# Two layers of spectral filter and mixer on one core: a half table negated on VectorE instead of loaded, layer 1's transform copies walked the other way, and three new instruction orders

## The chip, the cores and the metric

The kernel runs on one NeuronCore of a Trainium2 chip. The metric is the device time of one launch in microseconds (us). Before the change it was 348.33 us, the median of three runs (348.26 to 348.41). The engines are called as in the profile: PE (TensorE, the matrix engine; PEld is its weight load), DVE (VectorE), ACT (ScalarE), POOL (GpSimd) and SP (SyncE, which here only issues DMAs).

## What is computed

The input `x` has 2048 rows of 512 channels. The program applies block A, block B, block A, block B, with the same weights each time and a layer norm and a residual around each block.

```python
def _A_ref(x, w_r, w_i):
    X = rfft2(x, axes=(-2, -1))
    y = irfft2(X * (w_r + 1j * w_i), s=(S, D), axes=(-2, -1))       # S = 2048, D = 512
def _B_ref(x, w1, w2, w3, w4):
    h = gelu(layernorm(x) @ w1)                                     # w1: 512 x 512
    # the four quarters of h's channels are moved by +1, -1, +2, -2 rows
    x1 = x + shifted(h) @ w2                                        # w2: 512 x 512
    return x1 + gelu(layernorm(x1) @ w3) @ w4                       # w3: 512 x 1792, w4: 1792 x 512
x = x + _A_ref(layernorm(x));  x = x + _B_ref(layernorm(x))         # and both once more
```

## The kernel before

`x` stays on the chip as 16 rows q of a tile of 128 partitions by 512 channels (row number = 16 p + q). A layer is one block A and one block B. It has these stages, and in the order strings each step is a letter, the number of the piece, sometimes the engine that copies (V for DVE, A for ACT) and, behind a point, the bank of PSUM that it starts in:

- **p transform.** `Q` scales the table T by a row's 1/std, `O` multiplies two rows with it (`over_p`, or `over_p_plain`), `G` copies the result to the tile V. Of layer 1 this is done in `first_front`, together with the statistics (`s`, `i`, `f`, `S`, `J`), while `x` is still being loaded; of layer 2 it is done while layer 1's last products run.
- **The front of block A**, on 16 blocks b taken in ten units of one or two blocks: `d` (`over_d`, transform over the channels; `t` is its copy to the tile TV), `q` (`over_q`, with the tables TL; `x` is its copy to X), `p` (`weigh`, on DVE: X times the filter W, to PB), `b` (`back_q`, with the tables TR; `m` is its copy into the tile hT). Only after the last `m` can `D` start.
- **The back of block A:** `D` (`back_d`; `Y` is its copy), `P` (`back_p`), `a` (`add_x`, on DVE: adds x and sums), `s` (squares, ACT), `r`, `e`, `i`, `c` (statistics of four rows, on POOL, ACT and DVE), `n` (normalise), `T` (a DMA transpose of two rows, issued by SP).
- **Block B:** `v` (w1) with gelu `h` (ACT), `u` (w2 on shifted columns), `f` (DVE add), `k` (squares), `E` (residual), `R`, `o` (normalise, DVE or ACT), `U` (DMA transpose), `w` (w3) with gelu `g`, and `W` (w4) with `A` (add on DVE). In layer 1, `B`, `j`, `S`, `J` are the next layer's statistics, and `L` (`permute`, DVE) re-sorts W for layer 2. In layer 2 `y` (`store`) issues a row's store on SP.

Every engine runs its instructions in the order of the program, and the program is written out by hand in three strings: ORDER_0 for `first_front`, ORDER_A for layer 1, ORDER_B for layer 2. What an engine waits for follows from the data, from the bank of PSUM that a product is written to (it must have been copied out), and from buffers: TV and Y share four, X has two, so that `x` of one unit waits for `p` of the unit two before.

The tables come by DMA. POOL's queue (`load_rest`, L179 to L197) loads FA, TL and half 0 of TR, issues a DMA that doubles a quarter of W, waits on a one-element copy (`gate`, L191) for the last scaled table of `first_front`, then makes the second form of TL in two halves (`turn_TL`: a scaling of 1.66 us and a copy of 0.75 us for each), with three more doublings and half 1 of TR between and behind them. `back_q` multiplies planes k and k+1 of TR, so it needs the three planes A, B and -A of the blocks' half: blocks 0 to 7 use half 0, blocks 8 to 15 half 1. Half 0 comes with two planes, and DVE makes the third (`N0`, `negate`); half 1 is loaded with all three.

Layer 1 keeps TV with the two halves h interleaved (f h), as W comes; layer 2, after the permutes, keeps it as (h f). So layer 1's copy `t` has to interleave.

Of the kernel before, what the change touches and what calls it, by code (L numbers as in the profile page):

```python
# [28 lines left out]
def dft_tables():  # L29

    p = np.arange(P)
    pair = lambda j, s: (j if s == 0 else 64 - j) if j else 32 * s
# [6 lines left out]
    T = T.reshape(P, P)  # L50
# [104 lines left out]
def load_all(K, A_x, A_w_r, A_w_i, B_w1, B_w2, B_w3, B_w4):  # L155
# [24 lines left out]
    def load_rest(after):  # L180
        q = nc.gpsimd
        load_TL = lambda k: q.dma_start(K.TL[:, 0, 8 * k:8 * k + 8], dram["TL"][:, 8 * k:8 * k + 8])
        load_TR = lambda k: q.dma_start(K.TR[:, 0:2 + k, 16 * k:16 * k + 16], dram["TR"][:, 0:2 + k, 16 * k:16 * k + 16])
# [636 lines left out]
P6.2 s3 D2.0 s0 s1 a7 s7 a6 s6 D5.3 D4.6 r0 e0 Y2V P4.5 Y5A Y4A i0 n0V n1V P5.0 a4 s4 a5 s5 P11.2 D7.4 r1 P10.6 T0 Y7A  # L820
P8.3 e1 n3V n2V c1 T1 a11 a8 i1 D6.0 Y6A n5V P9.4 s11 P14.7 n4V n6V a9 n7V T2 P15.5 P12.3 a10 s8 a15 s9 a14 s10 P13.0
L0 v0.1 h0 a12 a13 v1.5 h1 T3 r2 c2 v3.4 n11V s12 c0 n10V T5 n8V n9V h3 s15 v2.3 h2 u0.5 L8 u3.0 u2.7 f0 L2 s14 f3
u1.5 f1 s13 r3 n12V n14V n15V f2 T4 v5.2 n13V h5 v4.1 u4.5 f4 E1 h4 u7.6 u6.1 f7 E3 u5.4 T7 k1 k0 f6 f5 k3 k2 E5 R0 c3
T6 v7.5 h7 u15.7 E0 v6.0 h6 E6 E4 u8.4 k7 o0V k5 o1V f15 E2 k6 o2V u10.3 o3V f10 k10 u12.7 u11.0 f8 u14.1 f14 U0 U1
u9.2 f9 k9 k8 w2.4 g2 f12 L9 E9 k4 R1 f11 k11 R2 w5.6 E11 g5 w4.2 g4 w1.0 u13.4 E8 o8V g1 o9V w3.5 g3 f13 E10 o10V
w0.1 g0 E7 o4A o7V w6.3 g6 W2.2 z0 o5V o6V A2 W3.7 A3 W1.6 A1 B1 W0.2 U3 U4 U2 E14 A0 w8.6 L13 B3 j3 g8 k14 o11V w12.1
g12 U5 w13.6 g13 w7.3 g7 w9.6 g9 k15 w10.3 g10 w18.0 w15.3 E12 g18 g15 w14.6 g14 w16.0 L11 w11.3 g11 g16 B2 W6.2 E13
W4.0 A6 w20.5 k13 L5 A4 B4 L12 W7.0 g20 w17.4 k12 R3 g17 o13A W5.1 A5 w19.5 g19 W9.2 o12V U6 j1 A7 B7 L15 j7 E15 j2 L7
o15V B6 W8.1 j6 B0 B5 j5 L3 W10.7 j0 S0 A10 B10 o14A U7 A9 j10 w25.4 g25 B9 Q2 j4 j9 A8 B8 L1 S1 Q1 Q4 w24.6 g24 W11.0
# [10 lines left out]
s5 a7 s7 a3 r1 P2.0 a2 P0.7 a0 s3 P1.3 a1 s2 e1 i1 n4V D5.4 D7.1 D4.6 Y5A P11.3 P10.0 n5V D6.4 n7V n6V s0 s1 r0 Y7A e0  # L840
Y4V P8.6 P9.2 T2 P14.1 a10 i0 c1 n2V n3V Y6A s10 a11 n1V P15.0 n0A s11 a9 a8 s9 s8 c0 r2 T3 P13.7 a13 P12.5 a12 T1
v3.3 h3 v2.6 h2 s12 n10V T0 v1.2 n8V n9V T4 v0.4 s13 n11V h1 u3.7 a14 T5 h0 a15 u1.6 f1 u0.0 s15 u2.4 f2 s14 r3 n14V
n15V T7 n12V v5.2 h5 v4.1 h4 u4.5 n13V E1 k1 u6.4 f3 E3 f0 E0 u7.3 k2 u5.7 k3 k0 c2 f7 T6 v6.2 h6 v7.1 h7 E2 f5 u13.6
R0 u12.0 E7 o2V u14.7 o3V o1V f6 o0V c3 f12 U0 f13 u15.2 f15 k15 f4 f14 E14 E15 E6 k13 k12 u9.0 f9 u10.1 k14 U1 w2.4
g2 w4.6 k4 f10 R3 k10 E13 w0.1 g0 w6.3 E12 o12A g4 w1.1 g1 g6 w3.5 g3 w5.1 g5 u11.5 E4 k5 f11 W2.3 E11 o13V o14A k7 U6
o15A k11 W1.4 A1 k6 R1 u8.2 A2 f8 k9 k8 R2 o6V U7 w25.6 g25 w22.3 o4V E10 o10A g22 E5 o5V w21.0 W3.2 A3 g21 w24.5 g24
o11V E9 w26.0 g26 o7V E8 w27.2 w23.5 U2 o8A g23 g27 W0.0 A0 y0 y2 W12.6 W14.7 A14 A12 W15.3 y3 o9V U3 w8.5 g8 y1 w11.1
g11 U4 A15 y15 w12.3 w10.0 g12 g10 U5 W13.7 A13 w7.1 w16.3 g16 g7 y13 w20.5 g20 w9.0 g9 w13.2 g13 W7.4 A7 y12 W4.6
# [33 lines left out]
```

## Time and profile before

The profiled execution took 348.26 us. Its span, the time from first to last recorded instruction, is 346.5 us, which leaves 1.76 us around it. It is 0.07 us below the median.

| stretch, us from the span's start | what runs | PE busy | DVE busy | ACT busy |
|---|---|---|---|---|
| 0 to 18.7 | loads of x, statistics, p transform of layer 1 | 16.16 | 14.40 | 13.93 |
| 18.7 to 38.4 | front of block A, layer 1 | 19.19 | 17.82 | 17.46 |
| 38.4 to 53.1 | back of block A, layer 1 | 14.47 | 12.37 | 12.48 |
| 53.1 to 179.4 | block B, layer 1, up to the last w4 product | 125.81 | 73.32 | 58.39 |
| 179.4 to 183.5 | rest of layer 2's p transform | 4.02 | 3.92 | 3.38 |
| 183.5 to 203.1 | front of block A, layer 2 | 19.16 | 18.01 | 17.26 |
| 203.1 to 218.4 | back of block A, layer 2 | 14.51 | 11.14 | 14.24 |
| 218.4 to 343.1 | block B, layer 2 | 124.16 | 36.48 | 54.81 |
| 343.1 to 346.5 | last add and store | 0 | 0.40 | 0 |

Busy times of PE overstate: the end of a matmul is modelled, and one that streams 512 columns is written down with 379 ns where the next one starts 216 ns later. In the two stretches of block B the matmuls follow each other at that distance; in the other stretches three engines hand work round, and the chain of waits, which goes back from the last instruction to whatever released each step, changes its engine every microsecond or so. The clock that was granted to PE is 1.0 in every stretch.

### The profile page before, as it was taken

The page shows a single profiled execution, that of the slowest core. Times are in us where ns is not written, and L with a number is a line of the kernel's source. Part 1 is how long each engine was busy: PE and PEld are TensorE (multiplying, and loading weights), DVE is VectorE, ACT ScalarE, POOL GpSimd, SP SyncE. Part 2 cuts the span into 40 slices and gives each one's busy share as a digit, 9 for nine tenths or more (in the row PEclk, how much of TensorE's full clock was granted, in tenths as well). Part 3 has the DMA queues.
Part 4 walks back from the last instruction along what each step waited for, and adds up shares of the span by engine and source line. Part 5 has one row for each costly group of instructions (what it writes and reads, how often), then busy time and mean ns, then how long its engine had stood idle before and what let it go on. Part 6 is the DMA issues. An engine that isn't in the chain of part 4 may idle for free.

```text
span 346.5 us, 5563 instructions
## 1 busy us (share of the span) xinstructions
PE 337.5 (97%) x2116; PEld 190.0 (55%) x2134; DVE 187.9 (54%) x452; ACT 192.0 (55%) x342; POOL 65.2 (19%) x158
## 2 busy tenths in 40 slices
...
GB/s 265 290 328 246 359 132 111 80 63 7 49 45 30 0 2 0 55 38 1 0 2 0 2 2 53 95 88 50 23 2 61 30 45 104 19 30 17 45 23 53
DMA packets 45337, 24.64 MB, mean 71 GB/s; under 512 B 34944, under 2 KB 42240, under 8 KB 45312
## 3 DMA queue, kind: packets, MB, share of 16 engines
q1 hardware_dynamic: 43904, 20.00, 23.6%
...
q14 instruction: 9, 0.07, 0.1%
...
## 4 chain that ended last, share of the span: by engine, by line
PE 80%; DVE 8%; ACT 5%; DMA 4%; issue 2%; DVEq 0%; SPq 0%; ACTq 0%
PE ps L686 28%; PE ps L706 27%; PE ps L635 8%; PE ps L651 8%; PE ps L511 3%; DVE x_state L603 3%; DMA xT<-xn 2%; ACT V L152 2%; PE ps L583 2%; DVE PB L554 2%; PE ps L535 1%; DMA x_state<-in_A_x_dram 1%; DVE hT L150 1%; ACT X L152 1%; DMA T<-tab_T 1%
## 5 line engine op out<-in xcount | busy, mean ns | idle before, releaser
L693 ACT ACTIVATE gT<-ps 128x1024 bf16<-128x1024 f32 x56 | 56.3, 1022 | 93.9 <-PE ps L686 93.7
L686 PE MATMUL ps<-xT,w 128*128 128x512 bf16 x448 | 99.3, 379 | 0.1
L706 PE MATMUL ps<-w,gT 128*128 128x512 bf16 (+1 forms) x464 | 97.8, 366 | 0.6
L712 DVE TENSOR_TENSOR x_state<-ps,x_state 128x512 bf16<-128x512 f32 (+1 forms) x34 | 22.1, 657 | 108.6 <-PE ps L706 106.9
L706 PEld LDWEIGHTS <-gT 128*128 128x128 bf16 x476 | 46.5, 98 | 49.9
L686 PEld LDWEIGHTS <-w 128*128 128x128 bf16 x448 | 43.7, 98 | 52.9 <-DMA xT<-xn 0.6
L659 DVE SCALAR_TENSOR_TENSOR xn<-xn,ln_c,ps 128x512 bf16<-128x512 bf16 x32 | 23.2, 744 | 21.4 <-PE ps L651 13.1
L635 PE MATMUL ps<-xT,w 128*128 128x512 bf16 x128 | 28.8, 379 | 0.9 <-DMA xT<-xn 0.9
L651 PE MATMUL ps<-w,hT 128*128 128x512 bf16 x122 | 28.6, 379 | 0.3
L285 ACT ACTIVATE junk<-xn 128x512 bf16<-128x512 bf16 x32 | 19.7, 619 | 10.1 <-DVE xn L659 10.1
L642 ACT ACTIVATE hT<-ps 128x512 bf16<-128x512 f32 x32 | 18.1, 601 | 11.8 <-PE ps L635 11.8
L603 DVE SCALAR_TENSOR_TENSOR x_state<-ps,x_state 128x512 bf16<-128x512 f32 x32 | 20.5, 686 | 5.1 <-PE ps L595 5.1
L273 DVE BATCH_NORM_STATS2 ln_st<-x_state 128x6 f32<-128x512 bf16 (+1 forms) x31 | 20.2, 667 | 3.6 <-DMA x_state<-in_A_x_dram 3.2
L635 PEld LDWEIGHTS <-w 128*128 128x128 bf16 x128 | 12.4, 98 | 16.0 <-issue 1.6
L291 POOL TENSOR_SCALAR ln_mv<-ln_s 128x4 f32<-128x4 f32 x16 | 4.9, 304 | 85.3 <-DVE x_state L603 73.2
L651 PEld LDWEIGHTS <-hT 128*128 128x128 bf16 x128 | 12.5, 98 | 15.1
L554 DVE TENSOR_TENSOR PB<-X,W 128x2048 bf16<-128x2048 bf16 (+1 forms) x20 | 19.6, 1010 | 0.7 <-ACT X L152 0.5
L285 ACT ACTIVATE xn<-x_state 128x512 bf16<-128x512 bf16 x32 | 19.9, 624 | 0.2 <-DVE x_state L603 0.2
L293 POOL TENSOR_TENSOR ln_mv<-ln_s,ln_t 128x4 f32<-128x4 f32 x16 | 3.5, 217 | 75.4 <-ACT junk L285 70.0
L583 PE MATMUL ps<-G,hT 128*128 128x256 bf16 x128 | 15.4, 272 | 0.9 <-DVE hT L150 0.8
L565 PE MATMUL ps<-TR,PB 128*128 128x128 bf16 x256 | 16.1, 219 | 0.1
L565 PEld LDWEIGHTS <-PB 128*128 128x128 bf16 x256 | 14.8, 98 | 1.5 <-issue 1.2
...
## 6 DMA issues: line engine op xcount, KB each, us to landing
w<-in_B_w_dram SPq DMA_DIRECT2D x2, 1792.0 KB, 12.1
...
```

The source lines that it names most:

```text
L285: K.nc.scalar.activation(out, src, ACT.Square, bias=0.0, scale=D ** -0.5, accum_out=self.s[:, i, 1:2])
L554: nc.vector.tensor_tensor(t, X.pop(u)[:, 0:2 * n].unsqueeze(1).to_broadcast([P, 2, 2 * n, 256]), K.W[:, :, 2 * u:2 * u + 2 * n, 1:257], op ...
L565: nc.tensor.matmul(oh, lhsT=pab[u][:, k, 2 * (b - u) + h, F * P:(F + 1) * P], rhs=K.TR[:, k:k + 2, 2 * b + h], start=(k == 0), stop=(k == 1))
L583: nc.tensor.matmul(o[:, i, e * 256:(e + 1) * 256], lhsT=M[:, F, e, 2 * m + i, :], rhs=K.G[:, F, e, :], start=(F == 0 and e == 0), stop=(F ...
L603: nc.vector.scalar_tensor_tensor(K.x[:, q, :], ps.pop(("P", q)), 1.0, K.x[:, q, :], op0=ALU.mult, op1=ALU.add, accum_out=ln[g].s[:, i, 0:1])
L635: nc.tensor.matmul(o[:, i], lhsT=K.w1[:, t, j * P:(j + 1) * P], rhs=xT[g][:, :, t, :], start=(t == 0), stop=(t == 3))
L651: nc.tensor.matmul(o, lhsT=K.hT[:, j, st:st + P], rhs=K.w2[:, j, :], start=(j == 0), stop=(j == 3))
L659: nc.vector.scalar_tensor_tensor(xn[:, q, :], xn[:, q, :], ln[q // 4].c[:, q % 4:q % 4 + 1], ps.pop(("u", n)), op0=ALU.mult, op1=ALU.add, ...
L686: nc.tensor.matmul(o[:, i], lhsT=K.w3[:, c, t * P:(t + 1) * P], rhs=xT3[g][:, :, c, :], start=(c == 0), stop=(c == 3))
L693: nc.scalar.activation(gT[g][:, 2 * j:2 * j + 2, :], ps.pop(("w", k)), ACT.Gelu_apprx_tanh, bias=0.0, scale=1.0)
L706: nc.tensor.matmul(o, lhsT=gT[g][:, t, i * P:(i + 1) * P], rhs=K.w4[:, t, d], start=(t == 0), stop=(t == 13))
L712: nc.vector.tensor_tensor(x, ps.pop(("W", n)), x, op=ALU.add)
```

## The change

Five things differ; the tiles, the matmuls and their number are the same.

1. The table TR is stored with two planes, and half 1 is loaded with two planes (512 KB, was 768 KB).
2. Layer 1 has a second `negate`, `N1`, on DVE, that makes the third plane of half 1.
3. Layer 1's copy `t` walks its elements in the order (h f) instead of (f h). The source in PSUM is then read in sequence and the destination in SBUF is written at every second element; before, the source was read at a jump of 128 elements and the destination written in sequence. What is stored where is the same.
4. All three order strings are replaced.
5. As the new ORDER_0 ends with `Q15A`, the last scaled table, for which POOL's `gate` waits, is made by ACT; before, it was `Q14V`, on DVE.

The number of zero matmuls ahead of the first p transform (35, `WAKE`) and the halving of one row of w4 by columns in each layer (`HALVES`) are the same in both kernels.

```diff
-    TR = np.concatenate([TR, -TR[:, :1]], axis=1)
...
-        load_TR = lambda k: q.dma_start(K.TR[:, 0:2 + k, 16 * k:16 * k + 16], dram["TR"][:, 0:2 + k, 16 * k:16 * k + 16])
+        load_TR = lambda k: q.dma_start(K.TR[:, 0:2, 16 * k:16 * k + 16], dram["TR"][:, :, 16 * k:16 * k + 16])
...
-            copy(K, tv[u][:].rearrange("p n (e f h) -> p (n e) f h", e=2, h=2),
-                 src.rearrange("p n (e h f) -> p (n e) f h", e=2, h=2), eng)
+            copy(K, tv[u][:].rearrange("p n (e f h) -> p (n e) h f", e=2, h=2),
+                 src.rearrange("p n (e h f) -> p (n e) h f", e=2, h=2), eng)
...
 ORDER_0 = """
-s0 s2 i0 s3 s1 i2 i3 f0 s4 S0 J0 i4 s5 Q1V Q0V Q3V Q2V s7 s6 i7 i6 s9 s11 O0 G0A f1 i9 S1 J1 s8 O1 G1A Q6A s10 Q7A i11
-O3 i8 i10 Q5A s13 s12 Q4A O2 S2 J2 i13 Q10V G3A i12 Q9V s15 Q11A O5 S3 Q8A s14 i15 G2A O4 i14 S4 J3 Q12V G5A J4 Q15A
-Q13V O6 Q14V G6A G4V O7 G7V O8 G8V G8A
+s0 s2 s3 i0 i2 i3 s1 f0 S0 s4 J0 Q2V Q3V O1 i4 s5 s7 s6 Q1A Q0A i7 i6 G1A f1 S1 O0 G0A s11 s10 i11 J1 Q6A i10 s8 s9
+Q7A Q4A i8 i9 s13 Q5A s12 S2 J2 i13 i12 Q10V O3 G3A Q11A O2 Q8V O5 Q9A s15 s14 S3 J3 i15 i14 G2A S4 Q13V Q12V J4 Q14V
+G5A Q15A O4 O6 G6A G4V O7 G7V O8 G8A G8V
 """
 ORDER_A = """
-X4.1 N0 d0.3 t0A d2.5 d1.7 t1A d4.0 t4A q0.2 x0A t2V q1.4 x1V p1 d10.6 d6.4 p0 t6V q2.1 t10A q4.6 x2A p2 x4A d12.3
-b1.0 q6.1 p4 q10.6 t12A m1V b3.3 m3V x6A d8.4 d14.2 d15.0 x10A b5.6 t8A q8.4 p6 t14V t15A q12.0 b2.7 p10 m2V q14.2 m5A
-x8A x12A q15.4 b0.6 m0A b10.7 m10A b4.1 m4A p8 b6.0 p12 m6V x14A p14 b11.7 x15A b9.1 p15 b13.6 m11A m9V m13A b7.3
-b12.5 m12A b8.2 m8A b14.7 m14A m7V b15.5 m15A m15V D1.1 Y1V D0.5 D3.3 P2.7 a2 P3.2 a3 Y0A P0.1 a0 Y3A P7.4 P1.7 a1 s2
...
-w21.2 g21 Q6 w22.6 j8 A11 L4 Q0 Q7 B11 j11 g22 L10 O0.3 w26.1 L14 g26 S2 Q11 G0A Q3 w23.6 w27.0 Q9 G0V g23 O1.2 G1A
-Q10 G1V g27 W12.5 A12 O3.0 B12 W15.6 j12 Q5 G3A G3V A15 O2.2 G2A B15 Q8 j15 G2V S15 J15 Q15 W13.5 A13 B13 S12 W24.4
-A24 j13 S13 J12 Q12 B24 J13 W14.5 Q13 A14 B14 O4.0 G4A O15.2 j14 S14 O5.6 G15V G15A O6.4 J14 Q14 O14.2 G4V G5A X3.7
-G14V L6 G6A X4.1 G14A
+N0 X4.6 d0.5 t0V d1.7 t1A d2.2 t2A q0.0 x0V p0 q1.6 d4.4 d10.0 q2.2 x1A t10A p1 t4V d6.6 t6V q4.4 x2A x4A p2 p4 d12.1
+t12A q10.6 q6.3 d14.0 d8.1 t14V x6A p6 x10A b0.3 t8A b3.5 b2.6 m2A b5.4 b1.0 p10 m3A m1V m0V m5A q8.1 x8A q12.6 N1
+d15.5 t15V b6.0 b4.3 b7.2 x12A q15.6 m4A p8 p12 q14.4 m6A x14A b10.3 b9.0 m10A m9V b11.1 m7A x15A p14 p15 m11A b8.4
+b12.5 m12A b13.0 m13A m8V b14.1 m14A b15.6 m15V m15A D1.3 Y1A D0.0 Y0A D3.5 Y3A P2.3 a2 s2 P3.1 P0.0 a3 s3 a0 s0 P1.2
+a1 s1 r0 D2.3 Y2V D4.6 Y4A P6.5 a6 P7.2 a7 P4.1 e0 a4 c0 i0 n0V s6 s7 D5.5 Y5A s4 n1V P5.0 T0 a5 s5 n3V n2V P8.7 D7.2
+Y7A P9.6 a9 P11.4 a11 r1 e1 c1 D6.0 i1 n5V Y6A n4V P10.4 a10 s11 P15.3 n6V s9 n7V s10 a8 a15 P14.5 a14 P12.1 s8 P13.2
+T1 v0.6 r2 v1.3 s15 c2 h0 a13 h1 T2 a12 n9V T3 v3.5 s12 n8V T4 h3 n11V v2.3 u0.0 h2 s13 u1.4 n10V s14 r3 c3 u3.5 f1 T5
+k1 v5.3 h5 f3 k3 v4.1 h4 f0 n15V n13V n12V u2.7 n14V f2 T6 k0 u6.6 f6 u4.1 E1 E2 k2 k6 f4 T7 u7.4 u5.0 f5 v7.1 h7 R0
+E3 o3A f7 v6.0 u8.3 f8 o2V h6 u11.4 o1A E4 u9.0 u15.5 E0 o0V f15 u13.3 k8 f9 f13 k9 f11 u10.1 k5 L15 E7 E5 k4 u12.2 E6
+k7 R1 U1 f10 k11 o6V f12 u14.3 U0 L13 w3.4 w6.6 g6 L4 w1.1 g1 g3 o5V f14 k10 w0.6 w2.0 g2 g0 L12 w5.2 g5 o7V o4A E8
...
+w25.6 Q5 O2.4 B9 g25 W11.3 A11 w23.0 g23 w26.2 G2A B8 Q2 O1.6 B11 G2V g26 G1A G1V w22.0 g22 O0.2 G0A j10 G0V w27.4 g27
+W12.7 L7 j11 j9 O3.5 W15.4 j8 A12 B12 G3A G3V A15 B15 S2 Q10 z0 j15 S15 Q8 J15 j12 W13.2 Q15 W24.5 Q9 W14.3 A13 B13
+j13 S13 S12 Q11 A24 J13 Q13 O4.0 G4A J12 B24 Q12 A14 B14 j14 S14 O15.6 G15V G15A J14 Q14 O5.4 G5A O6.2 G4V O14.6 G14V
+G6A G14A X4.5 X3.4 L6
 ORDER_B = """
-d1.1 d4.3 t1V d15.7 t15V d8.0 t8V t4A q1.2 x1A p1 q4.6 x4A p4 d12.4 q15.2 t12A d10.6 x15A p15 t10A q8.0 q12.4 x12A
...
-W6.4 A6 w14.0 w15.3 g15 W5.2 g14 w18.0 A4 A5 g18 w17.6 g17 y7 y5 y6 w19.4 g19 W9.2 A9 W10.5 y4 y9 A10 y10 W8.0 A8
-W11.4 W20.6 A11 A20 y8 y14 y11 y20 z0
+d4.5 t4A d1.3 d8.1 t1V t8A q4.6 x4V q1.3 x1A p1 d15.5 t15A d12.2 t12A d10.6 t10A p4 q15.0 x15V p15 q8.4 q12.2 x12A x8V
...
+y12 y14 W4.3 A7 w20.4 g20 w18.6 g18 w14.4 y3 w16.6 g16 g14 W5.0 A5 y7 W8.4 A4 W11.2 A11 y11 W10.5 A10 y10 W9.7 y2 A8
+z0 A9 y4 y5 y9 y6 W20.0 A20 y8 y20
 """
```

In numbers of copies, the front of block A is split as follows (V means DVE, A means ACT; a unit of two blocks is a copy of 1024 elements, of one block 512):

| front | kernel | `t` on V | `x` on V | `m` on V |
|---|---|---|---|---|
| layer 1 | before | 2, 6, 14 | 1 | 1, 2, 3, 6, 7, 9, half of 15 |
| layer 1 | after | 0, 4, 6, 14, 15 | 0 | 0, 1, 8, 9, half of 15 |
| layer 2 | before | 1, 8, 15 | 8, 10 | 2, 7, 10, 14, half of 15 |
| layer 2 | after | 1 | 4, 8, 10, 15 | 7, 10, 11, 14, half of 15 |

More of the change, by code (lines that the diff above doesn't have):

```diff
@@ L820 @@
[L820 to L829, printed above, removed]
@@ new lines @@
+k1 v5.3 h5 f3 k3 v4.1 h4 f0 n15V n13V n12V u2.7 n14V f2 T6 k0 u6.6 f6 u4.1 E1 E2 k2 k6 f4 T7 u7.4 u5.0 f5 v7.1 h7 R0
+E3 o3A f7 v6.0 u8.3 f8 o2V h6 u11.4 o1A E4 u9.0 u15.5 E0 o0V f15 u13.3 k8 f9 f13 k9 f11 u10.1 k5 L15 E7 E5 k4 u12.2 E6
+k7 R1 U1 f10 k11 o6V f12 u14.3 U0 L13 w3.4 w6.6 g6 L4 w1.1 g1 g3 o5V f14 k10 w0.6 w2.0 g2 g0 L12 w5.2 g5 o7V o4A E8
+E12 w4.5 g4 W2.4 A2 W3.1 A3 W1.3 A1 k13 B1 L8 U2 U3 w8.0 g8 w9.3 g9 L1 w10.1 g10 W0.4 A0 B0 E14 j1 E11 w7.6 g7 B3 L9
+w11.0 w12.6 g11 g12 E15 R2 E10 o10A o11A U5 w13.4 g13 W7.7 W6.5 E9 W4.3 o9A k15 W5.6 A4 B4 o8A U4 A5 w15.3 w16.0 A6
```

26 lines of the change are left out of this document (14 added, 12 removed).

## The prediction

> **What bounds the kernel now.** I read the page, then busy time by stretch, then the chain of waits, then the engines' own timelines in the stretches where PE is not the bound. About 0.2% (0.7 us) is what a measurement of this kernel can tell from no change.
>
> ```profile
> span 346.5 us, 5563 instructions
> PE 337.5 (97%) x2116; PEld 190.0 (55%) x2134; DVE 187.9 (54%) x452; ACT 192.0 (55%) x342; POOL 65.2 (19%) x158
> ```
> ```profile
> 18.70:38.40 19.70, 19.19 (x258) 16.14 (x257) 17.82 (x23) 17.46 (x26) 5.34 (x7) 1.00 0.86 289
> 53.10:179.40 126.30, 125.81 (x616) 59.65 (x626) 73.32 (x190) 58.39 (x101) 25.08 (x55) 1.00 0.16 32
> 183.50:203.10 19.60, 19.16 (x256) 15.99 (x257) 18.01 (x22) 17.26 (x27) 0.00 (x0) 1.00 0.01 2
> 218.40:343.10 124.70, 124.16 (x581) 57.56 (x590) 36.48 (x94) 54.81 (x95) 19.11 (x48) 1.00 0.20 44
> ```
> The columns of the second fence are stretch, length, then busy time (and instructions) of PE, PEld, DVE, ACT and POOL, clock, DMA share and GB/s. The two block-B stretches, 251 of 346.5 us, are PE without a gap, and the change leaves every matmul in place: nothing can be won there, only lost. All can move in the other 95 us. In the two fronts of block A (19.7 and 19.6 us) DVE and ACT are busy for 17 to 18 us each, so the order decides. The DVE timeline of layer 1's front:
>
> ```profile
> 18.68 0.79 DVE L770 TENSOR_SCALAR TR<-TR 128x1024 bf16<-128x1024 bf16 x1
> 20.25 1.22 DVE L150 CAST TV<-ps 128x1024 bf16<-128x1024 f32 x1 [0.78 <-PE ps L511]
> 22.11 0.69 DVE L150 CAST X<-ps 128x512 bf16<-128x512 f32 x1 [0.63 <-PE ps L535]
> ...
> 25.56 2.37 DVE L554 TENSOR_TENSOR PB<-X,W 128x2048 bf16<-128x2048 bf16 x2 [0.29 <-ACT X L152]
> ...
> 36.60 1.66 DVE L150 CAST hT<-ps 128x512 bf16<-128x512 f32 x3
> ```
> DVE idles 0.78 + 0.63 + 0.29 us at the start and then not at all until 38.26; `D` starts at 38.41. So in layer 1's front DVE is the bound, behind a start with 1.7 us of slack.
>
> **Part 1, the start (0 to 18.7).** The same statistics run, but two scaled tables go from DVE (0.87 us for four, 0.22 each) to ACT (1.69 us for four, 0.42 each). DVE has 0.44 us less, ACT 0.84 more; ACT idles 1.02 us until 6.52, 0.91 until 8.94 and about 0.9 before 11.06, which covers it. Following both queues step by step: `G1A` at 8.7 instead of `G0A` at 8.94, `Q15A` 16.8 to 17.2, the last copies of V end at about 18.5 instead of 18.76. I take -0.15; bounds -0.44 (all of DVE's saving) and +0.4 (ACT's extra less DVE's).
>
> **Part 2, POOL's queue.** The gate now waits for `Q15A`:
>
> ```profile
> 16.59 0.17 POOL L191 COPY gate<-Tq 1x2 bf16<-1x2 bf16 x1 [4.17 <-DVE Tq L379]
> 16.85 1.66 POOL L233 TENSOR_SCALAR TL<-TL 128x512 bf16<-128x512 bf16 x1
> 18.43 0.75 POOL L234 COPY TL<-TL 128x512 bf16<-128x512 bf16 x1
> ...
> 19.80 1.66 POOL L233 TENSOR_SCALAR TL<-TL 128x512 bf16<-128x512 bf16 x1
> ...
> 23.90 0.77 POOL L183 DMA_DIRECT2D TR<-tab_TR  x1
> ```
> Gate at 17.35 instead of 16.59: +0.75 for all behind it, the first turned half of TL ready at 19.95, the second at 23.0, the doublings of W at 19.95, 23.0 and 23.6, half 1 of TR issued at 24.3 (+0.4, as the 0.59 us that POOL waited for the last load of W before 23.29 is gone). Who waits: `q0` needs the first half; PE gets to it after three units of `d`, 18.6 + 16 x 0.109 = 20.35: 0.4 spare. `p4` needs the first doubling, 19.95 + 0.65 + 4.5 (median to landing) = 25.1; DVE gets there at 26.4. `N1` needs half 1 of TR: it landed 6.8 us after issue; a third of the bytes less is at most 0.9 us at 289 GB/s, so 30.2 to 31.1, and DVE gets to `N1` at 31.5. Cost 0, cover 0.4 us; if half 1 lands later, DVE itself stands, and with it the whole front.
>
> **Part 3, layer 1's front.** DVE by queue, before: N0 0.79, `t` 2.9, `x` 0.6, `p` 9.2, `m` 3.95, together 17.4. After: N0 and N1 1.5, `t` 4.1, `x` 0.6, `p` 9.2, `m` 2.75, together 18.2: +0.8. (A copy of 1024 elements holds DVE for 1.14, of 512 for 0.60, `p` of two blocks for 1.13; ACT's are 0.92 and 0.50.) ACT stays at 17.4: 1.1 of `t` less, 1.1 of `m` more. The +0.8 meets the 1.7 us of slack: `t0` is on DVE directly behind N0 (18.5 to 19.3, then 19.9), where before it waited 0.78 for a unit of two blocks. Worked through: `x0` 20.75, `p0` 21.4, `p1` 22.05, `t4` 22.65, `t6` 24.15, and from there DVE has no gap: 1.14 + 2.26 + 0.6 + 2.26 + 1.2 + 0.71 + 0.6 + 2.26 + 0.6 + 1.2 + 0.6 = 13.4, 37.6; half of m15 waits for its product until 37.75 and ends at 38.1. ACT ends at 38.3. `D` starts at 38.3: -0.1, of which -0.15 was part 1's. So this part costs +0.05. Bounds: -0.8 (all slack used, ACT as early) and +0.8 (none used).
>
> The other walk of `t`: the trace has no copy out of PSUM with a destination at every second element. The nearest rows:
>
> ```profile
> L764 DVE COPY X<-W 128x1024 bf16<-128x1024 bf16 x16 | 10.9, 679 | 0.0
> ...
> L765 DVE COPY W<-X 128x1024 bf16<-128x1024 bf16 x16 | 6.9, 428 | 0.6
> ```
> From SBUF to SBUF, a jump by two costs 0.25 us per 1024 elements. But copies out of PSUM take 1.22 on DVE whether to TV in sequence or to V in runs of four, and before's jump in the source cost nothing (1.02 on ACT, as for X). I take 0; the upper end is 0.25 x 3.5 = 0.9 on DVE, the lower 0.
>
> POOL and DVE now work in SBUF at the same time: N0 runs in POOL's first scaling (17.6 to 19.2), `p0` and `p1` (21.4 to 22.65) in its second (20.65 to 23.0). Before, `p` began at 22.84, behind it. The nearest rows for a two-source DVE operation inside a POOL operation:
>
> ```profile
> 71.47 1.43 DVE L666 TENSOR_TENSOR x_state<-x_state,xn 128x512 bf16<-128x512 bf16 x4
> ```
> ```profile
> 70.93 1.04 POOL L309 TENSOR_TENSOR ln_r<-ln_ve,mhalf 128x4 f32<-128x4 f32 x1
> ```
> The four adds take 4 x 0.34 as elsewhere, though POOL's operation had begun 0.54 before: DVE was not held. I take +0.1; the bounds are 0 and +1.2 (below). The Trainium skill, page "SBUF — State Buffer", section "SBUF: two separate sides", says the opposite of a free overlap: POOL and a DVE operation with two SBUF inputs share a port pair as an exclusive lock, and whichever starts second waits for the whole instruction of the other. By the rule `p0` would wait from 21.4 to 22.3, and the sum would be about 0.8 higher. The row disagrees for a POOL operation of four elements; no row here shows one of 512.
>
> **Part 4, back of block A, layer 1.** From `D` to the second transpose's issue DVE has the same eight adds, one copy, two pairs of `n` and one reciprocal in another order: 11.05 as before. But the two transposes now follow each other by 1.25 instead of 1.87 us; in layer 2, where they do (213.12, 214.45), the second took 3.82 instead of 3.52. +0.3 at most; I take +0.15. Lower bound 0.
>
> **Part 5, block B, layer 1.** PE's total is the same. Three transposes come within 0.3 us of when PE asks: rows 12 to 15 for `v7` (issue 66.8 + 3.5 = 70.3, PE at 70.5), rows 6 and 7 for `v3` (56.45, PE at 56.7), and `U0` for the first `w`: `o0V` now stands behind f8, o2, E4, E0 on DVE, U0 issued 77.4, landing 80.6 to 80.9, PE at 80.9. I take +0.15; bounds 0 and +0.9 (0.3 for each).
>
> **Part 6, the change of layers.** Behind the last w4 product ACT has one `right`, one root, two half and two whole copies in both orders: 3.4 us from 0.6 behind it, `d` 4.2 behind it. 0; bounds -0.2 and +0.3.
>
> **Part 7, layer 2.** Front: DVE and ACT have 16.6 and 17.5 us in both kernels (one `x` of 1024 and one of 512 to DVE, two `t` of the same sizes to ACT). ACT starts 0.44 earlier, as `d4` comes first, and loses it again in gaps before `t8`, `t12` and `x12`: `D` at 19.55 behind `d` against 19.61. Back: v at 15.25 behind `D` against 15.30. Together -0.1; bounds -0.44 and +0.5.
>
> **Part 8, the tail.** The stores of the last rows: y9 becomes ready 0.77 before PE's end, and y6 and y8 are now queued behind it, ahead of y20. Stores in a row are issued 0.38 and 0.48 apart (339.25, 339.63, 340.10), so y20 is issued 0.56 behind PE's end, ready at 0.49: +0.07, and two more stores of 128 KB are under way. I take +0.1; bounds 0 and +0.4.
>
> Sum: -0.15 + 0 + 0.05 + 0 + 0.1 + 0.15 + 0.15 + 0 - 0.1 + 0.1 = +0.3. Against the profiled execution, 346.5 + 1.76 = 348.26, that is 348.56; the median lies 0.07 above it. I predict **348.6**.
>
> **The rivals.** (a) *DVE and POOL hold each other up in layer 1's front, or N1 waits.* `p0` to 22.3 (+0.85), then `p1` against the 0.75 us copy: t6 ends 0.7 to 1.2 later and all behind it on DVE; or POOL is stretched by as much, half 1 of TR lands at 32 and N1 waits 0.5 to 0.8. For it: POOL's L318, 0.25 as a rule, took 0.74 beside DVE's L764. Against it: the four adds. It decides slower from 0.4 us on. +0.9 on the sum: 349.5 (348.9 to 350.2). (b) *The copy at every second element is slow,* or several transposes are late together: +0.9, 349.4 to 349.8. For: nothing measured covers it; against: PSUM as the source. (c) *The slack is worth more than I count:* DVE's and ACT's earlier starts survive, -0.44 at the start, -0.4 in layer 1's front and -0.4 in layer 2's, so -1.0 against before: 347.2. For: 1.7 us of idle DVE; against: two buffers of X, which tie ACT's copy to DVE's `p`. (d) *The change does not act,* as the loaded plane was hidden and block B is PE: 348.3; it falls in the forecast's case.
>
> **How the numbers follow.** The worked sum with (d), 347.8 to 349.0: 0.36. (a) 0.24, (b) 0.17, (c) 0.23. Slower by over 0.2% (above 349.0): (a), (b) and 0.03 of the first case, 0.44; faster (below 347.6): (c), 0.22; within: 0.34. Leaving out the outer tenths, the range is 347.2 to 350.2.
>
> **What would show it.** In the new trace: N0 at 18.5, `p0` at 21.4 of 0.6 us, POOL's L233 of 1.66 and not 2.2, N1 without idle before it, `t` of 1.02 and 1.22 as before, `D` at 38.3, v at 53.2 and, 126.3 us later, PE's end of layer 1, y20 issued 0.56 behind the last product. Wrong would be the prediction if DVE stands before N1 or `p0`, if TV copies lengthen, or if PE shows gaps before L635 and L686 inside block B.

## The result, and the profile after

The changed kernel takes 350.75 us, the median of six runs (350.07 to 351.59), against 348.30 for the kernel before in the same series (348.06 to 348.41). The ratio is 1.0073, with a 95% interval from 1.0059 to 1.0087: 2.45 us slower. The prediction was 348.6 with a range up to 350.2, so the result lies outside it. The profiled execution took 351.18 us, 0.43 above the median; its span is 349.4.

The page's first lines and the windows at the new stage bounds (columns as in the prediction):

```profile
span 349.4 us, 5584 instructions
PE 336.2 (96%) x2116; PEld 189.2 (54%) x2134; DVE 185.9 (53%) x444; ACT 199.4 (57%) x351; POOL 62.9 (18%) x158
```
```profile
18.90:39.90 21.00, 19.59 (x257) 16.01 (x258) 19.56 (x24) 18.20 (x26) 6.91 (x8) 1.00 0.78 272
39.90:55.60 15.70, 14.51 (x128) 12.39 (x128) 12.16 (x38) 14.60 (x34) 5.59 (x18) 1.00 0.80 191
55.60:182.40 126.80, 125.90 (x615) 59.56 (x625) 69.84 (x183) 61.01 (x104) 21.00 (x51) 1.00 0.17 31
186.60:206.30 19.70, 19.03 (x256) 16.12 (x257) 17.68 (x22) 17.64 (x27) 0.00 (x0) 1.00 0.01 2
206.30:220.90 14.60, 14.18 (x129) 12.49 (x130) 11.71 (x32) 12.66 (x29) 2.44 (x10) 1.00 0.21 38
```
Layer 1's front (first fence line of the windows) is 1.3 us longer, and DVE is busy in it for 19.56 us where it was 17.82. The back of layer 1 is 1.0 longer with PE's busy time unchanged, so PE waits there. Layer 2's back, the last line, became 0.7 shorter. The stage lengths below go by the first matmul of each stage in the trace, of one profiled execution each ("block B 1" runs to the first `d` of layer 2; "tail" is from the start of the last w4 product's last matmul). The differences add up to 2.9, that of the two profiled spans:

| kernel | start | front 1 | back 1 | block B 1 | front 2 | back 2 | block B 2 | tail |
|---|---|---|---|---|---|---|---|---|
| before | 18.74 | 19.67 | 14.71 | 130.37 | 19.61 | 15.30 | 124.37 | 3.72 |
| after | 18.94 | 20.93 | 15.77 | 130.92 | 19.75 | 14.57 | 124.59 | 3.93 |
| after less before | +0.20 | +1.26 | +1.06 | +0.55 | +0.14 | -0.73 | +0.22 | +0.21 |

DVE's timeline in layer 1's front, after:

```profile
19.03 0.80 DVE L769 TENSOR_SCALAR TR<-TR 128x1024 bf16<-128x1024 bf16 x1
21.41 0.69 DVE L149 CAST X<-ps 128x512 bf16<-128x512 f32 x1 [0.95 <-PE ps L534]
22.14 2.29 DVE L553 TENSOR_TENSOR PB<-X,W 128x1024 bf16<-128x1024 bf16 x2
24.36 2.48 DVE L149 CAST TV<-ps 128x1024 bf16<-128x1024 f32 x2
...
33.24 0.42 DVE L769 TENSOR_SCALAR TR<-TR 128x1024 bf16<-128x1024 bf16 x1
```
The two `p` of one block (third line) take 2.29 us where the kernel before had 1.30:

```profile
22.84 1.30 DVE L554 TENSOR_TENSOR PB<-X,W 128x1024 bf16<-128x1024 bf16 x2
```
`N1` (last line of the timeline after) starts without idle time, so it does not wait for its load, and takes 0.42 us, while `N0`, the same instruction, takes 0.80. POOL's timeline over the same time:

```profile
17.64 0.17 POOL L190 COPY gate<-Tq 1x2 bf16<-1x2 bf16 x1 [1.82 <-ACT Tq L380]
17.89 1.66 POOL L232 TENSOR_SCALAR TL<-TL 128x512 bf16<-128x512 bf16 x1
19.48 0.97 POOL L233 COPY TL<-TL 128x512 bf16<-128x512 bf16 x1
...
21.06 1.66 POOL L232 TENSOR_SCALAR TL<-TL 128x512 bf16<-128x512 bf16 x1
22.63 1.30 POOL L233 COPY TL<-TL 128x512 bf16<-128x512 bf16 x1
...
25.12 0.73 POOL L182 DMA_DIRECT2D TR<-tab_TR  x1
```
`N0` starts inside the first scaling (17.89 to 19.55) and ends 0.28 behind its end. `p0` starts at 22.14, inside the second scaling (21.06 to 22.72), and ends at 23.32; POOL's copy, which takes 0.75 elsewhere, takes 1.30 beside it; `p1` ends 0.5 behind that copy. In these rows the two engines take turns.

The chain of waits around the first `v` and the first `w` of layer 1, and PE's waits between 38 and 90 us (us in total, times, longest):

```profile
50.87 0.16 DVE x_state L602
51.03 4.47 DMA xT<-xn
55.51 0.14 issue
55.65 1.45 PE ps L634 x6
```
```profile
78.95 0.94 SPq L622
79.89 0.05 issue
79.94 0.02 SPq L622
79.95 0.03 issue
79.98 3.69 DMA xT<-xn
83.68 0.14 issue
83.81 2.32 PE ps L685 x10
```
```profile
PE ps L634 <- DMA xT<-xn: 1.1, 1, 1.1
PE ps L582 <- ACT hT L151: 0.4, 1, 0.4
PE ps L685 <- DMA xT<-xn: 0.4, 1, 0.4
PE ps L594 <- DVE x_state L602: 0.2, 1, 0.2
```
PE waits 1.1 us for a transpose before `v` and 0.4 for another, U0, before the first `w`, inside block B. The kernel before waits for a transpose twice in its whole execution, each time at a `v` (L635), and not before its first `w`:

```profile
PE ps L635 <- DMA xT<-xn: 0.9, 2, 0.7
```
The four transposes ahead of `v` as SP issues them, first of the kernel before, then of the changed one; T0 is the first of each row, 9.18 and 9.80 us behind `D`:

```profile
47.59 6.75 SPq L623 DMA_TRANSPOSE xT<-xn  x4
49.67 6.58 SPq L622 DMA_TRANSPOSE xT<-xn  x4
```

### The profile page after: what moved, and what is told of

Read it like the earlier page. It is cut to its first block, busy times and chain, and to the rows that moved or that the text cites. A ratio compares the mean times of both kernels' runs of the same rounds, so it can differ in the third digit from the quotient of the medians.

```text
span 349.4 us, 5584 instructions
## 1 busy us (share of the span) xinstructions
PE 336.2 (96%) x2116; PEld 189.2 (54%) x2134; DVE 185.9 (53%) x444; ACT 199.4 (57%) x351; POOL 62.9 (18%) x158
## 4 chain that ended last, share of the span: by engine, by line
PE 76%; ACT 10%; DVE 5%; DMA 5%; issue 2%; SPq 0%; ACTq 0%; DVEq 0%
PE ps L685 28%; PE ps L705 27%; PE ps L634 8%; PE ps L650 6%; PE ps L510 3%; DMA xT<-xn 2%; ACT X L151 2%; ACT hT L151 2%; ACT V L151 2%; DMA x_state<-in_A_x_dram 2%; PE ps L582 2%; DVE x_state L602 1%; ACT xn L284 1%; PE ps L594 1%; PE ps L534 1%
## 5 line engine op out<-in xcount | busy, mean ns | idle before, releaser
L553 DVE TENSOR_TENSOR PB<-X,W 128x2048 bf16<-128x2048 bf16 (+1 forms) x20 | 20.4, 1059 | 0.1
L370 ACT ACTIVATE xn<-xn,ln_mr,ln_r 128x512 bf16<-128x512 bf16 x15 | 11.9, 806 | 9.3 <-DVE x_state L665 5.0
L510 PE MATMUL ps<-FA,V 128*128 128x256 bf16 x128 | 16.3, 273 | 0.3 <-ACT V L151 0.2
L307 POOL TENSOR_SCALAR ln_ve<-ln_mv 128x4 f32<-128x4 f32 x11 | 3.3, 302 | 72.0 <-DVE ln_mv L300 71.3
```

Of the source, the lines that this page charges most:

```text
L510: nc.tensor.matmul(oi[:, 1 - h], rhs=K.FA[:, t, h], lhsT=V[:, 2 * t + h, 2 * b:2 * b + 2].rearrange("d b q c -> d (b q c)"), start=(t == 0 ...
L553: nc.vector.tensor_tensor(t, X.pop(u)[:, 0:2 * n].unsqueeze(1).to_broadcast([P, 2, 2 * n, 256]), K.W[:, :, 2 * u:2 * u + 2 * n, 1:257], op ...
```

## The experiments

Each was timed beside the kernel before, and ratios are to that kernel. Stage lengths of all of them:

| kernel | start | front 1 | back 1 | block B 1 | front 2 | back 2 | block B 2 | tail |
|---|---|---|---|---|---|---|---|---|
| b_form | 18.95 | 20.29 | 15.06 | 130.36 | 19.61 | 15.32 | 124.25 | 3.69 |
| b_oA | 18.61 | 19.73 | 14.89 | 130.88 | 19.61 | 15.23 | 124.25 | 3.84 |
| b_o0 | 18.55 | 19.97 | 14.78 | 130.37 | 19.61 | 15.31 | 124.33 | 3.68 |
| b_oB | 18.57 | 19.67 | 14.95 | 130.37 | 19.76 | 14.67 | 124.50 | 4.05 |
| b_neg | 18.43 | 19.96 | 15.06 | 130.37 | 19.61 | 15.30 | 124.39 | 3.68 |
| a_form | 20.35 | 19.86 | 15.24 | 130.66 | 19.76 | 14.57 | 124.59 | 3.93 |
| a_gate | 18.84 | 20.09 | 15.76 | 131.00 | 19.76 | 14.58 | 124.58 | 3.89 |
| a_load | 18.44 | 20.56 | 15.33 | 131.01 | 19.76 | 14.59 | 124.57 | 3.90 |
| a_undo | 18.29 | 20.29 | 15.33 | 130.97 | 19.76 | 14.54 | 124.61 | 3.89 |
| a_TU | 18.70 | 20.92 | 14.94 | 130.37 | 19.75 | 14.58 | 124.58 | 3.89 |
| a_fix | 18.33 | 19.92 | 14.90 | 130.37 | 19.76 | 14.57 | 124.59 | 3.90 |
| b_back | 18.64 | 19.67 | 14.79 | 130.37 | 19.61 | 14.54 | 124.62 | 3.85 |

### One part alone, put into the kernel before

**b_form: the new walk of `t`.**

```diff
-            copy(K, tv[u][:].rearrange("p n (e f h) -> p (n e) f h", e=2, h=2), ...
+            copy(K, tv[u][:].rearrange("p n (e f h) -> p (n e) h f", e=2, h=2), ...
```


> The kernel before with one part of the change: layer 1's copy t writes every second element and reads PSUM in sequence. Theory A (the copies and the shared port): in the new kernel's trace ACT's t of 1024 elements took 1.32 to 1.36 us instead of 1.02, DVE's 1.24 instead of 1.22. Here ACT makes four t of 1024 and three of 512, so ACT gets 4 x 0.31 + 3 x 0.1 = 1.5 us more in layer 1's front, of which the idle time at its start covers a part: D starts 0.3 to 1.0 us later, time +0.3 to +1.0. Theory B (the new orders alone make the loss): the copies are hidden, time within 0.2 of before.

349.13 us, ratio 1.0017 (1.0007 to 1.0027). Front 1 went from 19.67 to 20.29. The walk costs, and it costs on ACT (the rows are shown with a_form below).

**b_oA: the new ORDER_A, without `N1`.**

```diff
-ORDER_A = (before)
+ORDER_A = (after, with " N1" taken out)
```


> The kernel before with the new ORDER_A alone, N1 left out (half 1 of TR still loaded with three planes), old walk of t, old start. Theory A: D starts within 0.4 us of before's 38.4, as ACT's copies are short and POOL's turn is 0.75 us earlier, with p0 and p1 meeting only the end of its second half; what is left are the first transposes (T0 0.6 us later behind D) and U0 (PE waits 0.4 us for it): time +0.5 to +1.2. Theory B: the order carries the loss, +2 to +2.5.

349.61 us, ratio 1.0032 (1.0019 to 1.0044). Front 1 is as long as before (19.73), the back +0.18, block B +0.51: that is the wait for U0. These stages give +0.7 us together, the times +1.1. The profiled execution, with a span of 347.0 us, is the shortest of the twelve; the median of their spans is 347.5, 1.0 above the kernel before (346.5). In it `v` came 5.1 us behind T0, earlier than in any other profiled execution, so the back of this row is likely shorter than usual.

**b_o0: the new ORDER_0,** with it the gate on ACT's `Q15A`.

```diff
-ORDER_0 = (before)
+ORDER_0 = (after)
```


> The kernel before with the new ORDER_0 alone: the gate waits for ACT's last table. Theory A: POOL's turn begins 0.8 us later, so p1 and p0 (22.84 in before) meet the copy of its second half, up to 23.0: one of them 0.3 us longer, time 0 to +0.4. Theory B: the start itself is longer, +0.4 to +0.8, and d starts later than 18.9.

348.67 us, ratio 1.0002 (0.9992 to 1.0012). Start -0.2, front 1 +0.3: POOL's turn comes 0.6 to 0.85 us later, `N0` takes 0.98 instead of 0.79 and the first `p` 0.85 instead of 0.69.

**b_oB: the new ORDER_B.**

```diff
-ORDER_B = (before)
+ORDER_B = (after)
```


> The kernel before with the new ORDER_B alone. In the new kernel's trace layer 2's front took 19.75 us instead of 19.61, its back 14.70 instead of 15.30, the tail 0.2 more. Both theories: that carries over, -0.6 + 0.14 + 0.2 = -0.3, between -0.6 and 0.

348.39 us, ratio 0.9994 (0.9983 to 1.0004). Back 2 is 0.63 shorter; front 2 gives back 0.15, block B 0.13 and the tail 0.33.

**b_neg: the load of two planes, and `N1`.**

```diff
-    TR = np.concatenate([TR, -TR[:, :1]], axis=1)
-        load_TR = ... K.TR[:, 0:2 + k, ...], dram["TR"][:, 0:2 + k, ...]
+        load_TR = ... K.TR[:, 0:2, ...], dram["TR"][:, :, ...]
 ORDER_A
-... b2.7 p10 m2V q14.2 ...
+... b2.7 p10 m2V N1 q14.2 ...
```


> The kernel before, with half 1 of TR loaded in two planes and its third plane made by DVE (N1 behind the seventh copy m of DVE's share). Theory 'DVE is the bound of layer 1's front': N1 alone on DVE takes 0.36 to 0.42 us and pushes all behind it, D 0.3 to 0.4 later, time +0.3 to +0.4 us (348.7), and N1 does not wait, as it comes at about 35 us and half 1 lands at 30 to 31. Rival 'the load of fewer bytes pays for it': 256 KB less on the queue, the weights behind it earlier, time 0 or below (348.1 to 348.4). A wait at N1 would show as idle time before L770.

348.81 us, ratio 1.0013 (1.0003 to 1.0022). `N1` took 0.42 without a wait and front 1 is 0.29 longer. No gain from the plane that is no longer loaded shows.

The five single parts add up to 1.0058; the whole change is 1.0073 (1.0059 to 1.0087).

### One part taken out of the changed kernel

**a_form: the old walk.**

```diff
-            copy(K, tv[u][:].rearrange("p n (e f h) -> p (n e) h f", e=2, h=2), ...
+            copy(K, tv[u][:].rearrange("p n (e f h) -> p (n e) f h", e=2, h=2), ...
```


> The changed kernel with the old walk (f h) of layer 1's copy t. In the kernel before the new walk alone cost 0.6 us (1.0017). Theory 'the walk slows ACT's five copies by 0.31 each and this adds to the rest': ACT's t back to 1.02 us, time -0.5 to -0.7 (350.1). Rival 'what bounds the changed front is DVE, held at p0 and p1, so that ACT's copies lie beside it': time unchanged within 0.2 (350.6 to 350.9). In either case DVE's t stays at 1.2 to 1.3 us.

350.33 us, ratio 1.0051 (1.0037 to 1.0064). Front 1 fell from 20.93 to 19.86, but not by the walk alone. This execution began 1.4 us late, and with that POOL's second scaling ended 3.05 us behind the first `d` instead of 3.79; the two `p` took 1.63 us instead of 2.29. So 0.66 of the fall is POOL's, and 0.41 is left for the walk. The copies by form, layer 1's front, first of the changed kernel, then of a_form (count, busy us, mean ns, idle before):

```profile
L151 ACT ACTIVATE TV<-ps 128x1024 bf16<-128x1024 f32 x4 | 5.3, 1332 | 0.8 <-PE ps L510 0.6
L149 DVE CAST TV<-ps 128x1024 bf16<-128x1024 f32 x2 | 2.5, 1293 | 0.0
```
```profile
L151 ACT ACTIVATE TV<-ps 128x1024 bf16<-128x1024 f32 x4 | 4.1, 1026 | 1.2 <-PE ps L510 1.2
L149 DVE CAST TV<-ps 128x1024 bf16<-128x1024 f32 x2 | 2.4, 1217 | 0.0
```
Writing every second element costs ACT 306 ns per copy of 1024, and DVE 76 ns. ACT has four of these and one of 512 (745 against 597 ns): 1.4 us of an engine that is busy for 18.2 of 21.0.

**a_gate: POOL's gate on DVE's `Q14`.**

```diff
-        last_T = K.Tq[q]
+        last_T = K.Tq[q] if q != 15 else last_T
```


> The changed kernel, with POOL's gate waiting for DVE's table Q14 in place of ACT's Q15. Theory 'POOL's late second turn holds DVE at p0 and p1': the gate comes 0.4 to 0.8 earlier (16.9 to 17.2), the second scaling ends at 22.0 to 22.3, p0 and p1 together take 1.5 to 1.9 instead of 2.37 us, D 0.4 to 0.8 earlier, time -0.4 to -0.8 (350.0 to 350.3). Rival 'p0 and p1 have slack, other engines set D': p0 and p1 shorter, but D within 0.15 and time within 0.2 (350.6 to 350.9).

350.36 us, ratio 1.0056 (1.0044 to 1.0069). The gate came at 16.83. The second scaling ran from 20.05 to 21.71, the two `p` from 22.05 took 1.45 instead of 2.29 us, and front 1 fell from 20.93 to 20.09, by as much:

```profile
22.05 1.45 DVE L553 TENSOR_TENSOR PB<-X,W 128x1024 bf16<-128x1024 bf16 x2
```
**a_load: half 1 of TR in three planes, no `N1`.**

```diff
+    TR = np.concatenate([TR, -TR[:, :1]], axis=1)
-        load_TR = ... K.TR[:, 0:2, ...], dram["TR"][:, :, ...]
+        load_TR = ... K.TR[:, 0:2 + k, ...], dram["TR"][:, 0:2 + k, ...]
 ORDER_A
-... x8A q12.6 N1 d15.5 ...
+... x8A q12.6 d15.5 ...
```


> The changed kernel, with half 1 of TR loaded in three planes and no N1. Theory 'N1 costs what it holds DVE, 0.42': D 0.3 to 0.4 earlier, time -0.3 to -0.4 (350.4). Rival 'N1 lies in slack, and the third plane's 256 KB cost the queue time': D the same, time within 0.2. The half lands 0.3 to 0.9 us later than with two planes; the products of blocks 8 to 15 would show a wait for a DMA if that were too late.

350.37 us, ratio 1.0057 (1.0044 to 1.0070). Front 1 fell by 0.37. By the times alone a_form, a_gate and a_load are not told from the changed kernel (the intervals overlap); the stages have to tell. Here they do not speak for `N1` as a cost: the two `p` took 1.93 us instead of 2.29, which is the whole fall, and where `N1` would have stood, behind two copies `m`, DVE now idles:

```profile
31.15 1.29 DVE L150 CAST hT<-ps 128x512 bf16<-128x512 f32 x2
32.73 0.74 DVE L150 CAST TV<-ps 128x512 bf16<-128x512 f32 x1 [0.29 <-issue]
```
This execution also shows how far the turn-taking goes; the columns are shortest, median and longest duration in ns and the starts of the two `p`:

```profile
L554 DVE TENSOR_TENSOR PB<-X,W x2: 695/980/1264, 21.6 to 22.3; 128x1024 bf16<-128x1024 bf16 x2
```
`p0` started at 21.62, 0.9 us into the second scaling (20.70 to 22.37), and was not held (0.69); `p1` met POOL's copy (22.27 to 23.04) and took 1.26.

### The parts together

**a_undo: old walk, early gate, three planes without `N1`;** the new orders stay. The edits are those of a_form, a_gate and a_load.

> The changed kernel with three parts undone together: the old walk of t, the gate on DVE's table Q14, half 1 of TR in three planes without N1; the three new orders stay. Theory 'the three add up': layer 1's front back to 19.7 to 19.9 us (20.9 in the changed kernel), time 349.4 to 349.7, which is the sum of what the new orders cost alone (1.0028 of the kernel before). Rival 'they pay for the same idle time, one undone part is enough': front at 20.0 to 20.3, time 350.1 to 350.4, as with each part undone alone.

349.78 us, ratio 1.0042 (1.0030 to 1.0054). Front 1 is 20.29, longer than b_oA's 19.73 with the same order: the rival's number, while the time lies nearer to the theory's. The reason is not the rival's. In this execution POOL's first doubling of W was issued 0.52 us after POOL had become free, so that the second scaling ran until 21.90 in spite of the early gate, and `p0` and `p1`, from 21.46, took 0.99 and 1.19. In a_fix, which is the same up to there, the scaling ended at 21.45, the two took 1.12 and 0.68, and front 1 is 19.92. What counts is where POOL's second turn lies beside the first `p`. The table has the kernel before and the eight kernels with the new ORDER_A ("first `p`" is `p1` in the kernel before, `p0` in the others; "rest" is front 1 less the time from the start of the first `p` to the end of the second):

| kernel | walk | `N1` | second scaling ends | POOL's copy ends | first `p` starts | the two `p` took | both | front 1 | rest |
|---|---|---|---|---|---|---|---|---|---|
| before | old | no | 21.47 | 22.14 | 22.84 | 0.69, 0.69 | 1.30 | 19.67 | 18.37 |
| b_oA | old | no | 21.51 | 22.19 | 21.82 | 0.87, 0.68 | 1.47 | 19.73 | 18.26 |
| a_fix | old | no | 21.45 | 22.13 | 21.51 | 1.12, 0.68 | 1.72 | 19.92 | 18.20 |
| a_undo | old | no | 21.90 | 23.06 | 21.46 | 0.99, 1.19 | 2.10 | 20.29 | 18.20 |
| a_form | old | yes | 23.40 | 24.07 | 23.55 | 1.03, 0.68 | 1.63 | 19.86 | 18.23 |
| a_load | new | no | 22.37 | 23.04 | 21.61 | 0.69, 1.26 | 1.93 | 20.56 | 18.63 |
| a_gate | new | yes | 21.71 | 22.39 | 22.05 | 0.84, 0.68 | 1.45 | 20.09 | 18.64 |
| a_TU | new | yes | 22.50 | 23.70 | 21.91 | 1.18, 1.19 | 2.29 | 20.92 | 18.63 |
| after | new | yes | 22.73 | 23.93 | 22.14 | 1.18, 1.19 | 2.29 | 20.93 | 18.64 |

In the new order the rest is 18.20 to 18.26 with the old walk and 18.63 to 18.64 with the new one, with or without `N1`, and whatever time both `p` take is added to it in full. So of the changed kernel's +1.26 in front 1 the `p` beside POOL are 0.99, the walk is 0.41, the order gives back 0.15, and `N1` costs nothing. In the old order `N1` costs 0.29 (b_neg: both `p` 1.30, rest 18.66) and the walk 0.61 (b_form: 1.30, rest 18.98).

**a_TU: two moves in the new ORDER_A.** The add `a4` behind T0, and the residual E0 and the two normalisations ahead of `f8`, on which DVE had waited 2.56 us.

```diff
-... e0 a4 c0 i0 n0V s6 s7 D5.5 Y5A s4 n1V P5.0 T0 a5 s5 ...
+... e0 c0 i0 n0V s6 s7 D5.5 Y5A n1V P5.0 T0 a4 s4 a5 s5 ...
-... R0 E3 o3A f7 v6.0 u8.3 f8 o2V h6 u11.4 o1A E4 u9.0 u15.5 E0 o0V f15 ...
+... R0 E3 o3A f7 E0 o0V o2V v6.0 u8.3 f8 h6 u11.4 o1A E4 u9.0 u15.5 f15 ...
```


> The changed kernel with two moves in ORDER_A: a4 (and s4) behind T0 instead of ahead of n0; and E0, o0V, o2V ahead of f8, so that DVE does them in its 2.56 us of idle time before f8. Theory 'T0 comes late by the add ahead of it, and U0 late by f8, o2, E4 and E0': T0 at 9.2 us behind D instead of 9.8, the first v 0.4 to 0.6 earlier, U0 issued at 5.5 to 6.0 us before the first w instead of 3.8, PE's wait of 0.38 us before L685 gone, time -0.8 to -1.0 (349.8). Rival 'the second transpose is held by the queue and not by when the first is issued': v at the same distance behind D, and only the 0.38 us are gained (350.4).

349.74 us, ratio 1.0039 (1.0027 to 1.0051): 1.0 us less than the changed kernel, as the first theory said. T0 was issued 9.20 behind `D` instead of 9.80, back 1 is 14.94 instead of 15.77, and block B has exactly the 130.37 us of the kernel before. PE's waits between 38 and 90 us:

```profile
PE ps L582 <- ACT hT L151: 0.4, 1, 0.4
PE ps L634 <- DMA xT<-xn: 0.2, 1, 0.2
PE ps L594 <- DVE x_state L602: 0.2, 1, 0.2
```
The 1.1 us before `v` are down to 0.2, and the 0.4 before the first `w` are gone.

**a_fix: a_undo and a_TU together.**

> The three undone parts and the two moves together, new orders otherwise. Theory 'all causes are named': front 19.8, v 14.7 to 15.2 behind D, no wait before L685, layer 2's back 0.6 shorter as in the changed kernel: time 348.3 to 348.8, level with the kernel before. Rival 'something else in the new orders costs': 349.2 or more, with PE gaps elsewhere in block B.

348.23 us, ratio 0.9996 (0.9987 to 1.0006): level with the kernel before, so the five edits together take out the loss, and nothing else in the new orders costs a time that these runs can tell. That `N1` had a part in the loss does not follow from this run; the table above says that it had none.

**b_back: the kernel before, with its own ORDER_B up to the last `m`, and the new one from `D` on;** rows 6 and 8 are stored ahead of row 9.

```diff
 ORDER_B
-... b15.1 m15A m15V D3.4 Y3A D2.6 D1.1 ... A11 A20 y8 y14 y11 y20 z0
+... b15.1 m15A m15V D3.6 Y3V D2.0 Y2A D1.2 ... A8 z0 A9 y4 y5 y6 y8 y9 W20.0 A20 y20
```


> The kernel before with its own ORDER_B up to the last m, then the new ORDER_B from D on, with the stores of rows 6 and 8 moved ahead of that of row 9. Theory 'the new back of layer 2 is worth 0.6 us, which its front (0.15), block B (0.13) and tail (0.27) give away': back 14.6 to 14.7 us instead of 15.3, tail 3.7 to 3.8 us behind the last w4 product instead of 4.0, time 347.7 to 347.9, faster than both. Rival 'the early v only moves a wait into block B, whose weights or transposes then come late': back shorter, but from v to the last product as much longer, time 348.2 to 348.5.

347.97 us, ratio 0.9988 (0.9979 to 0.9996): 0.4 us faster than the kernel before, and the fastest of all. Back 2 is 14.54 instead of 15.30, and 0.25 of it comes back in block B. The chain of waits there no longer goes over a DMA:

```profile
213.17 0.92 ACT Y L152
214.09 0.04 issue
214.13 3.65 PE ps L595 x32
217.78 0.86 PE ps L635 x4
218.65 0.03 issue
218.67 0.38 PE ps L635
```
PE goes from `P` into `v` without a pause; in the kernel before the chain had a transpose of 3.82 us there and PE waited 0.7:

```profile
214.45 3.82 DMA xT<-xn
```
In b_back, behind the first four matmuls of `v`, there is a gap of 0.2. Why the two transposes, issued at the same distance behind `D` (10.0 and 11.3 us), are done earlier in this order wasn't tested. The tail, 3.85, is 0.20 shorter than b_oB's, which has row 9 first, and 0.13 longer than that of the kernel before; but with the old end of ORDER_B it varies from 3.68 to 3.84 too.

## Why the prediction was wrong, by its own steps

- **Part 1, start: -0.15.** In the eight executions with the new ORDER_0 `d` begins at 18.29 to 20.35 (median 18.62), in the six with the old one at 18.43 to 18.95 (median 18.63): a gain of 0.15 can't be told. The changed kernel's own lay at 18.94, 0.20 later than before. In it the rows of x landed a median of 6.0 us after their issue, against 4.8 before; but in a_gate and a_TU they took 6.1 and 6.0, and `d` began at 18.84 and 18.70. What sets the start isn't shown.
- **Part 2, POOL's queue: 0.** The times of the queue were right (gate 17.35 said; 17.23 to 17.64 in four executions, 18.52 in a_form's, which began late), and no one waits for what POOL makes: `N1` doesn't either. The cost lies in what runs beside it, and the step looked for it in part 3 only.
- **Part 3, DVE's queue: +0.05.** That is right, for the order (b_oA: +0.06, of which 0.17 is time of the two `p` beside POOL) and for `N1`, which costs nothing in the new order. Only in the old order does it cost 0.29 (b_neg). That DVE alone bounds the front of the kernel before is not right: slower copies on ACT lengthened it by 0.6 (b_form).
- **Part 3, the walk: 0, bounds 0 to +0.9. This step failed.** The bound was priced on DVE by the nearest copy from SBUF to SBUF, and the value taken because the source in PSUM had borne a jump for nothing. Writing at a jump is another thing, and on another engine: ACT, whose rows the step did not price, pays 0.31 per 1024 elements. In the front that is +0.62 in the old order (b_form) and +0.41 in the new one (the last column of the table above).
- **Part 3, POOL beside DVE: +0.1, bounds 0 to +1.2. This step failed too.** It measured 1.0 on the two `p` of the changed kernel, and the earlier gate gives back 0.84 of the front (a_gate). The Trainium skill, page "SBUF — State Buffer", section "SBUF: two separate sides", states that POOL and a DVE operation with two SBUF inputs exclude each other, and the prediction's estimate by it was about 0.8 higher. It was set aside on the strength of four adds beside a POOL operation of four elements, the wrong row: a pair of 128 x 4 says little of one of 128 x 512. Two rows of the profile before pointed the other way. One the prediction names itself under rival (a): POOL's L318, 0.74 instead of 0.25 beside a DVE copy. The other is `N0` inside POOL's scaling at 0.79; that the same instruction takes 0.42 alone was seen only at `N1`. Of the nine executions that started the first `p` inside a scaling or copy of POOL, eight show it held (0.84 to 1.18 instead of 0.69), as the page has it; in a_load it started 0.9 us into a scaling and was not held, against the page.
- The front as a whole: taken out singly the three parts seem to give 1.07, 0.84 and 0.37, or 2.3 of a loss of 1.26. That is because a_form's and a_load's executions also had POOL's turn at another place beside the `p`. With the time of both `p` taken off, the terms add up: 0.99 + 0.41 - 0.15 + 0.
- **Part 4, transposes: +0.15. This step failed too.** The back became 1.06 longer. The step followed the second transpose's issue (11.05 behind `D`, then 11.16) as what `v` hangs on. It was the first one's issue that counted: 9.18 before, 9.80 after, as `a4` went ahead of it. `v` comes 5.5 to 5.9 us behind the first issue in the eight executions where the second follows by 1.87 us, and 5.1 to 6.0 in the six where it follows by 1.36. Issuing the second earlier wins next to nothing; of the 1.06, 0.62 is the first issue and 0.44 lies within that spread. As a_gate's back is as long (15.76), the 0.44 may be more than the chance of one execution; what makes the spread is not shown.
- **Part 5, block B: +0.15, bounds 0 to +0.9.** Measured +0.55, of which PE's wait for U0 is 0.4; with the two moves of a_TU all of it is gone. U0 was named and is right as a mechanism, and its size was not: issued at 79.98, 2.58 later than said, 2.45 of it because `v` is later by that, it landed after 3.69 instead of 3.2 to 3.5. `v7` and `v3` did not wait.
- **Part 6: 0,** right: from the first `w` to layer 2's `d` 102.75 us, against 103.61 before, where one `u` (0.86 us) still lay behind that `w`.
- **Part 7, layer 2: -0.1.** Front +0.14 and back -0.73, of which 0.2 comes back in block B: -0.4, inside the bounds. The front was said to win 0.06, and the back's gain was seen only as 0.05.
- **Part 8: +0.1,** measured +0.21: y20 is issued 0.14 later, behind the two stores, and lands 0.21 later. (The 340.10 in this step's row of times is not the issue of a store; the one behind 339.63 is issued at 342.27.)

Rivals (a) and (b) were both true, (a) without its half on `N1`, (b) in both its halves. Each was priced as if the others were false, +0.9 each, and the range ended a little behind one of them. Their sum, 350.4, was nearest to what came out. As they are independent (one is DVE beside POOL, the other a copy's pattern and a queue), the range should have reached there. (The three terms of rival (c) add up to -1.24 and not to -1.0.)
